# Attention with packed keys and a routed feed-forward: the second batch's routing read ahead of its last softmax steps, two subtractions on GpSimd

## The chip, the cores and the metric

The kernel runs on one core of one Trainium2 chip. The metric is the device time of one execution in microseconds, as the median of the runs shown. The profile is one such execution; its times are counted from the start of its span.

## The reference

Eight batches of 576 tokens with 8 heads of 64. An attention over 32 packed rows per head, then a top-1 mixture of experts on the result (D = 512, E = 8 experts, F = 1024):

```python
p_packed = sm_attn(p, k, v)              # 32 packed rows per head
out = sm_attn(q, p_packed, p_packed)     # softmax over the 32 rows
x = out.transpose(0, 2, 1, 3).reshape(B * S, H * D)
xn = x / (norm(x) + 1e-6); en = emb / (norm(emb) + 1e-6)
logits = xn @ en.T / tau
idx = argmax(logits, axis=1)             # the token's expert
gate = softmax(logits)[idx]
out[token] = gate * (relu(x @ w1[idx]) @ w2[idx])
```

## The kernel before

**Precision.** The feed-forward runs as fp32r with a high and a low part: `AT[:, 0]` is the attention's second softmax rounded (`high`, ScalarE), `AT[:, 1]` is the rest (`low`, one subtraction). The same split is made for the first weights times the packed rows (`G`, `w1_rows`, L854 and L855) and for the second weights (`w2s`, `split_w2`, L816 and L817). Each product takes three passes (`PASSES`).

**Batches and stages.** For each batch an expert is guessed from the sum of the logits, the whole batch is computed for it, and a loop behind it serves tokens that fall to another expert (with these inputs it has nothing to do). `ffn` is the backbone: for a batch it does two halves of the hidden layer (L923), the output of the tail tokens (L951, four times 24 matmuls), and that of the first 256 tokens (L969, two times 24). Between the pieces of `ffn` of batch b the steps of batch b + 1 are issued: attention part one (`att1`), the guess, `att2` (query scores, softmax, transposes), the routing (`route`), and then the keys of batch b + 2. While batch 0 is in `ffn`, a table of letters, `PLAN`, says after each yield of `ffn` what is issued: `a` a step of batch 1's attention, `r` one of batch 0's routing, `g` one of batch 0's gates, `w` a split of second weights. For later batches a rule does this.

**The softmax of att2** works on two halves of 288 tokens. For each: `unpack` (transposes out of PSUM), `biggest`, `shift`, `expo` on ScalarE, `total` (L597 to L599), `norm` (L603), `turn` (a transpose into `at`, L606), `high` (L609, ScalarE), `low` (L613). Its order stands in a list; for batch 1 (`early`) the list is rearranged a little.

**The routing** multiplies `at` with the packed rows and their logits (L681), in two groups of tokens: the first 256, all in the first half, with 32 matmuls, and the other 320 with 40. Each group fills both buffers `pt` of a PSUM pool that has two. A group is read tile by tile: VectorE sums the logits (L695), ScalarE squares the values and sums them up (L699). When the second group is read, the token's expert is found on VectorE (L706 to L723), and `counts` (L732, L735) sums it over the tokens on TensorE.

**The gates** (`gates`, L743 to L770) need an inverse root of the squares' sum. For batch 0 its three rounds (L102, L104, L111, L112) and two closing steps (L749, L750) run on GpSimd; VectorE, ScalarE (an exponential, L757) and VectorE again make the gate, and 16 small copies on ScalarE (L778) lay it out for the tail tokens, whose output L1267 multiplies.

**What the next batch needs.** `w1_rows` (L841) fills the same two `pt` buffers; each half is read by two casts on ScalarE (L854) and two subtractions on VectorE (L855). The key scores of batch b + 2 (L259) fill them again: the first four matmuls the one, the next four the other.

Every engine works through its instructions in the order in which they are issued.

Of the kernel before, what the change touches and what calls it, by code (L numbers as in the profile page):

```python
# [23 lines left out]
def kernel(  # L24
# [193 lines left out]
    def alternate(a, b):  # L218

        while a or b:  # L220
            for g in (a, b):
                if g:
                    try:
                        yield next(g)
                    except StopIteration:
                        a, b = (None, b) if g is a else (a, None)

    def idle(n):
        for _ in range(n):
            yield  # L230
# [317 lines left out]
    def att2(x, after=None, first=False, early=False):  # L548

        def eng(name, hf):  # L550
            i = ("S0", "S1", "N0", "N1", "L0", "L1").index(name + str(hf))
            if early and name + str(hf) in POOLED:
                return nc.gpsimd
            return nc.gpsimd if first and ENG[i] == "p" else nc.vector

        AT = sb.tile([P, 2, NG, S], F32R, name="AT", tag="AT")
        x.AT = AT
        NB = HS // 32
        both = slice(0, NG)
        sts, mxs, sums = [], [], []  # L560
        if first:
            at = x.at = sb.tile([P, NG, S], F32, name="at1", tag="ot", bufs=1)
        else:
            at = x.at = sb.tile([P, NG, S], F32, name="at", tag="at")

        def rows_of(t, gs):
            return t[:, gs].rearrange("p g (a j) -> p g a j", j=32)

        def spread(t, gs):
            n = gs.stop - gs.start  # L570
            return t[:, gs].unsqueeze(3).broadcast_to([P, n, NB, 32])

        def unpack(hf, gs=both):
            if gs.start == 0:
                sts.append(sb.tile([P, NG, HS], F32, name="st", tag="st", bufs=2))
            for g in range(gs.start, gs.stop):
                nc.vector.transpose(sts[hf][:, g], x.s2[hf][g])

        def biggest(hf, gs=both):
            if gs.start == 0:  # L580
                mxs.append(sm.tile([P, NG, NB], F32, name="mx2", tag="mx2", bufs=1))
            nc.vector.tensor_reduce(
                mxs[hf][:, gs], rows_of(sts[hf], gs), axis=AX.X, op=ALU.max
            )

        def shift(hf, gs=both):
            t = rows_of(sts[hf], gs)
            eng("S", hf).tensor_tensor(out=t, in0=t, in1=spread(mxs[hf], gs), op=ALU.subtract)  # L588

        def expo(hf, gs=both):  # L590
            nc.scalar.activation(sts[hf][:, gs], sts[hf][:, gs], AF.Exp, scale=SCALE)  # L591

        def total(hf, gs=both):
            if gs.start == 0:
                sums.append(sm.tile([P, NG, NB], F32, name="s2", tag="s2", bufs=1))
            t = sums[hf][:, gs]
            nc.vector.tensor_reduce(t, rows_of(sts[hf], gs), axis=AX.X, op=ALU.add)  # L597
            nc.vector.tensor_scalar(out=t, in0=t, scalar1=1e-9, scalar2=None, op0=ALU.add)
            nc.vector.reciprocal(t, t)  # L599

        def norm(hf, gs=both):
            t = rows_of(sts[hf], gs)
            eng("N", hf).tensor_tensor(out=t, in0=t, in1=spread(sums[hf], gs), op=ALU.mult)  # L603

        def turn(hf, gs=both):
            nc.vector.transpose(at[:, gs, hf * HS : (hf + 1) * HS], sts[hf][:, gs])  # L606

        def high(hf, gs=both):
            nc.scalar.copy(AT[:, 0, :, hf * HS : (hf + 1) * HS], at[:, :, hf * HS : (hf + 1) * HS])  # L609

        def low(hf, gs=both):
            cs = slice(hf * HS, (hf + 1) * HS)
            eng("L", hf).tensor_tensor(  # L613
                out=AT[:, 1, :, cs], in0=at[:, :, cs], in1=AT[:, 0, :, cs].bitcast(F32),
                op=ALU.subtract,
            )

        def softmax():
            order = (
                (unpack, 0), (biggest, 0), (shift, 0), (unpack, 1), (biggest, 1), (total, 0),  # L620
                (shift, 1), (norm, 0), (turn, 0), (total, 1), (low, 0), (norm, 1), (turn, 1),
            )
            if early:
                order = (order[0], order[3], order[1], order[2], *order[4:])
            if first:
                names = dict(
                    U=unpack, B=biggest, S=shift, X=expo, T=total, N=norm, R=turn, H=high, L=low
                )
                groups = {"": both, "a": slice(0, 1), "b": slice(1, 2)}
                order = [(names[t[0]], int(t[1]), groups[t[2:]]) for t in ORDS.split()]  # L630
            for step, hf, *gs in order:
                step(hf, *gs)
                if step is shift and not first:
                    expo(hf)
                if step is turn and not first and not hf:
                    high(hf)
                yield
            if first:
                return
            if not after:  # L640
                high(1)
                low(1)
                return
            high(1)
            yield from idle(1 if early else 4)
            steps = route(x)
            if early:
                yield next(steps)
                next(steps)
                yield next(steps)  # L650
                low(1)
                yield
                yield from steps
                yield from after
                return
            yield next(steps)
            next(steps)
            low(1)
            yield from idle(3)
            yield from alternate(after, steps)  # L660

        yield from softmax()


# [348 lines left out]
    order = {bi: n for n, bi in enumerate(seq)}  # L1013
# [220 lines left out]
    def store_main(b):  # L1234
# [60 lines left out]
        "qssq", "sssssssss", "sss", "ss", "ss", "ssG", "", "sG", "ssa", "ssa",  # L1295
# [5 lines left out]
    )  # L1301
    POOLED = ()
    DBL = 8
    LAG = 2

# [6 lines left out]
    with tc.manual_schedule():  # L1312
# [41 lines left out]
        for b in range(B):  # L1354
            after = bat[b + 1] if b + 1 < B else None
# [24 lines left out]
    with tc.If(n_rest > 0):  # L1380
        with tc.For_i(0, B, 1) as b:
            nb = nc.values_load(rest_i[0:1, ds(b, 1)], min_val=0, max_val=S)
            with tc.If(nb > 0):
                x = Batch()
# [98 lines left out]
```

## Time and profile before

| | us |
|---|---|
| median of 3 runs | 439.41 |
| the runs | 438.62, 439.89, 439.41 |
| the profiled execution | 438.68 |
| its span | 437.1 |
| TensorE (matmuls) busy | 417.7 |
| VectorE busy | 312.6 |
| ScalarE busy | 217.9 |
| GpSimd busy | 137.5 |

The profiled execution's mean granted TensorE clock is 0.985 of the full 2.4 GHz. A share of busy time is a mean over stages. The stage around this change lies between 60 and 95 us: batch 0 is in its output products, batch 1 in its softmax and routing. In the rows below PE is TensorE's matmuls, DVE VectorE, ACT ScalarE, POOL GpSimd; an instruction's idle time and what ended it stand in brackets.

### The profile page before, as it was taken

What the parts mean: (1) busy time and instruction counts of PE and PEld (TensorE: products, weight loads), DVE (VectorE), ACT (ScalarE), POOL (GpSimd) and SP (SyncE); (2) the same over time, 40 slices, a digit from 0 to 9 for tenths busy, and PEclk for the clock granted to TensorE, in tenths of its full rate; (3) what the DMA queues carried; (4) which work ended last, traced back from release to release, by engine and by line L of the source; (5) the groups of instructions that cost most, each with busy time, mean ns of one, the idle gap of its engine ahead of it and who ended that gap; (6) DMA issues with size and microseconds to landing.
All of it is one profiled execution on the core that took longest, in us unless ns stands there. A gap on an engine that the chain in (4) does not pass through costs nothing.

```text
span 437.1 us, 12609 instructions
## 1 busy us (share of the span) xinstructions
PE 417.7 (96%) x4802; PEld 351.7 (80%) x4803; DVE 312.6 (72%) x982; ACT 217.9 (50%) x652; POOL 137.5 (31%) x185
## 2 busy tenths in 40 slices
PE   7889996998999999999999999999999999999994
PEld 5646885688896889869896899859896898869993
DVE  4468678667996689868897589867897589656420
ACT  2456733665535744367534754367344664456300
POOL 2438743053212514044122424044041524035000
PEclk9899999799999999999999999999999999999998
DMA  7999989687897669965897668965798603731032
GB/s 198 294 292 281 247 232 264 189 188 172 251 359 206 152 192 305 310 167 128 249 362 204 153 178 270 326 180 135 215 335 246 170 16 102 287 74 36 2 63 53
DMA packets 47908, 88.36 MB, mean 202 GB/s; under 512 B 10904, under 2 KB 29400, under 8 KB 47840
## 3 DMA queue, kind: packets, MB, share of 16 engines
q1 hardware_dynamic: 39456, 57.83, 49.3%
q0 software_dynamic: 8000, 29.43, 19.5%
q8 instruction: 40, 0.66, 0.6%
q10 hardware_dynamic: 384, 0.21, 0.2%
q14 instruction: 28, 0.23, 0.2%
HBM read 78.00 MB, written 9.44 MB: 200 GB/s over the span
## 4 chain that ended last, share of the span: by engine, by line
PE 81%; DMA 7%; DVE 5%; ACT 3%; issue 1%; POOL 1%; SPq 1%; DVEq 0%; POOLq 0%; ACTq 0%
PE pf L951 24%; PE pf L969 19%; PE pf L923 19%; PE pt L259 4%; PE pt L681 4%; DMA nat<-in_v 3%; PE pt L841 3%; DMA nat<-in_q 2%; PE pt L384 2%; DMA nat<-in_k 2%; PE pt L364 1%; ACT scr L699 1%; PE pf L902 1%; PE pf L1179 1%; SPq L1251 1%
## 5 line engine op out<-in xcount | busy, mean ns | idle before, releaser
L817 POOL TENSOR_TENSOR w2s<-w2r,w2s 128x512 fp32r<-128x512 f32 x64 | 82.2, 1287 | 134.3 <-ACT w2s L816 133.0
L951 PE MATMUL pf<-hT,w2s 128*128 128x320 f32 x768 | 120.6, 312 | 0.0
L951 PEld LDWEIGHTS pf<-hT,w2s 128*128 128x128 f32 x768 | 113.0, 188 | 4.3 <-issue 3.3
L923 PE MATMUL pf<-AT,G 128*128 128x288 f32 x720 | 103.9, 298 | 0.1
L923 PEld LDWEIGHTS pf<-AT,G 128*128 128x128 f32 x720 | 97.3, 188 | 4.8 <-issue 2.3
L969 PE MATMUL pf<-w2s,hT 128*128 128x512 f32 (+1 forms) x408 | 96.7, 390 | 0.0
L969 PEld LDWEIGHTS pf<-w2s,hT 128*128 128x128 f32 x408 | 73.0, 191 | 20.8 <-issue 5.9
L926 DVE SCALAR_TENSOR_TENSOR hT<-pf,hT 128x288 fp32r<-128x288 f32 x128 | 56.3, 445 | 25.1 <-ACT hT L925 25.1
L925 ACT ACTIVATE hT<-pf 128x288 fp32r<-128x288 f32 x128 | 51.3, 415 | 39.2 <-PE pf L923 38.3
L699 ACT ACTIVATE scr<-pt 128x256 f32<-128x256 f32 (+1 forms) x80 | 29.8, 379 | 39.8 <-DVE lg L695 39.8
L816 ACT CAST w2s<-w2r 128x512 fp32r<-128x512 f32 x64 | 39.2, 624 | 6.3 <-issue 6.3
L792 POOL DMA_DIRECT2D w1t<-in_moe_w x14 | 10.7, 767 | 79.7 <-DVE st L588 75.1
L855 DVE TENSOR_TENSOR G<-pt,G 128x512 fp32r<-128x512 f32 x28 | 19.3, 690 | 17.4 <-ACT G L854 17.4
L778 ACT COPY gt<-gate 32x2 f32<-32x2 f32 (+1 forms) x128 | 24.6, 192 | 6.3 <-DVE gate L763 4.2
L1258 DVE STREAM_TRANSPOSE ot<-pf 128x320 f32<-128x320 f32 x32 | 16.0, 501 | 13.7 <-PE pf L951 11.5
L854 ACT CAST G<-pt 128x512 fp32r<-128x512 f32 x28 | 16.5, 589 | 17.6 <-DVE G L855 13.2
L609 ACT CAST AT<-at 128x576 fp32r<-128x576 f32 x16 | 10.8, 673 | 26.5 <-DVE at L606 25.4
L591 ACT ACTIVATE st<-st 128x576 f32<-128x576 f32 (+1 forms) x17 | 11.2, 658 | 24.0 <-issue 19.4
L681 PEld LDWEIGHTS pt<-ppf,at 32*64 32x64 f32 x1152 | 15.7, 136 | 8.9 <-ACT scr L699 4.4
L695 DVE TENSOR_REDUCE lg<-pt 128x8 f32<-128x32 f32 (+1 forms) x80 | 11.4, 175 | 15.8 <-PE pt L681 11.1
L681 PE MATMUL pt<-ppf,at 32*64 32x72 f32 x1152 | 18.4, 241 | 4.3 <-ACT scr L699 4.0
L289 DVE STREAM_TRANSPOSE kt<-nat 128x576 f32<-128x576 f32 x28 | 21.2, 762 | 0.0
(179 smaller groups left out, 491.9 us busy)
## 6 DMA issues: line engine op xcount, KB each, us to landing
nat<-in_k SPq DMA_DIRECT2D x112, 140.0 KB, 3.4
nat<-in_q SPq DMA_DIRECT2D x112, 140.0 KB, 5.0
w1t<-in_moe_w POOLq DMA_DIRECT2D x14, 1024.0 KB, 8.9
w2r<-in_moe_w POOLq DMA_DIRECT2D x28, 512.0 KB, 12.6
nat<-in_v SPq DMA_DIRECT2D x32, 160.0 KB, 3.8
out<-ot SPq DMA_DIRECT2D x28, 160.0 KB, 3.5
nat<-in_v SPq DMA_DIRECT2D x32, 128.0 KB, 3.7
out<-o SPq DMA_DIRECT2D x62, 64.0 KB, 1.7
```

The source lines that it names most:

```text
L289: nc.vector.transpose(kt.rearrange("p (n i) -> p n i", i=32), t)
L681: nc.tensor.matmul(pts[h // 2][64 * (n % 2) : 64 * (n % 2) + 64, at : at + XW], x.at[32 * h : 32 * h + 32, g, 64 * n : 64 * n + 64], x.ppf ...
L699: nc.scalar.activation(scr[:r], v[:, :, :D], AF.Square, accum_out=sss[:r, m, c : c + 1])
L778: copy(dst[32 * a : 32 * a + 32, k : k + HB * (n - 1) + 1 : HB], src[32 * k : 32 * k + 32, NCT : NCT + n],)
L816: nc.scalar.copy(hi, raw)
L817: eng.tensor_tensor(out=lo, in0=raw, in1=hi.bitcast(F32), op=ALU.subtract)
L855: nc.vector.tensor_tensor(out=x.G[:, 1, g, fs], in0=src, in1=x.G[:, 0, g, fs].bitcast(F32), op=ALU.subtract,)
L923: nc.tensor.matmul(pf[:, :HS], w, r, start=(n == 0), stop=(n == len(ops) - 1))
L925: nc.scalar.activation(hT[:, 0, f, cs], pf[:, :HS], AF.Relu)
L926: nc.vector.scalar_tensor_tensor(out=hT[:, 1, f, cs], in0=pf[:, :HS], scalar=0.0, in1=hT[:, 0, f, cs].bitcast(F32), op0=ALU.max, op1=ALU.s ...
L951: nc.tensor.matmul(pf[:, : S - TL], x.w2s[f][:, m, mt * P : mt * P + P], hT[:, a, f, TL:], start=(n == 0), stop=(n == len(ops) - 1),)
L969: nc.tensor.matmul(pf[:, :w], hT[:, a, f, c * P : (c + 1) * P], x.w2s[f][:, m, at : at + w], start=(f == 0 and i == 0), stop=(f == NF - 1 ...
```

## The change

For batch 1 alone, four things. The list of softmax steps ends before the last `norm` and `turn`; the routing's first group is issued and read there, and the two steps follow, then the second group. Both `low` subtractions go to GpSimd. In `PLAN` the steps of the gates of batch 0 (`g`) move, so that the gate's exponential and copies come behind the squares of batch 1. Some of the steps `a` come earlier or in twos and threes.

```diff
             if early:
-                order = (order[0], order[3], order[1], order[2], *order[4:])
+                order = (order[0], order[3], order[1], order[2], *order[4:9], *order[9:11])
...
             if first:
                 return
+            if early:
+                steps = route(x)
+                yield next(steps)
+                next(steps)
+                yield next(steps)
+                norm(1)
+                yield
+                turn(1)
+                high(1)
+                yield
+                yield next(steps)
+                low(1)
+                yield
+                yield from steps
+                yield from after
+                return
             if not after:
                 high(1)
                 low(1)
                 return
             high(1)
-            yield from idle(1 if early else 4)
+            yield from idle(4)
             steps = route(x)
-            if early:
-                yield next(steps)
-                next(steps)
-                yield next(steps)
-                low(1)
-                yield
-                yield from steps
-                yield from after
-                return
...
-        "ra", "ra", "ra", "ra", "a", "a", "ra", "ga", "ga", "ga",
-        "ga", "rga", "", "ga", "ga", "ga", "g", "ga", "gar", "ga",
-        "aa", "a", "a", "a", "a", "a", "a", "a", "", "",
+        "ra", "ra", "ra", "ra", "a", "a", "rga", "ga", "ga", "g",
+        "g", "", "", "aaa", "ar", "", "g", "", "aar", "aa",
+        "agg", "agggg", "a", "a", "a", "a", "", "", "", "",
     )
-    POOLED = ()
+    POOLED = ("L0", "L1")
```

`POOLED` names the softmax steps that batch 1 gives to GpSimd. Lines behind the first part are 7 higher in the changed kernel (L681 becomes L688).

How it moves instructions. TensorE, from the last products of the tail tokens on; `ppf,at` are batch 1's routing groups, `oh,ones` the counts of batch 0, `w1t,T` the next batch's first weights. Before:

```order
L681 MATMUL pt<-ppf,at 64x72 x32
L951 MATMUL pf<-hT,w2s 128x320 x8
L969 MATMUL pf<-w2s,hT 128x512 x6
L681 MATMUL pt<-ppf,at 64x72 x40
L969 MATMUL pf<-w2s,hT 128x512 x3
L732 MATMUL pu<-oh,ones 1x32
L735 MATMUL pu<-oh,ones 1x8
L969 MATMUL pf<-w2s,hT 128x512 x18
L841 MATMUL pt<-w1t,T 32x512 x16
```

and with the change:

```order
L688 MATMUL pt<-ppf,at 64x72 x32
L958 MATMUL pf<-hT,w2s 128x320 x8
L976 MATMUL pf<-w2s,hT 128x512 x9
L688 MATMUL pt<-ppf,at 64x72 x40
L739 MATMUL pu<-oh,ones 1x32
L742 MATMUL pu<-oh,ones 1x8
L976 MATMUL pf<-w2s,hT 128x512 x18
L848 MATMUL pt<-w1t,T 32x512 x16
```

The first group stays; the second comes three matmuls later and has the counts right behind it.

ScalarE, from the softmax's last exponential to the next batch's splits; `scr,ss` are the squares, `lgt` the gate's exponential, `gt` its copies. Before:

```order
L609 CAST AT<-at 128x2x288 x2
L757 ACTIVATE lgt<-lgt 128x40
L699 ACTIVATE scr,ss<-pt 128x256 x4
L778 COPY gt<-gate 32x3 x2
...
L699 ACTIVATE scr,ss<-pt 128x256 x2
L699 ACTIVATE scr,ss<-pt 64x256 x2
L816 CAST w2s<-w2r 128x512
L854 CAST G<-pt 128x512 x2
```

and with the change:

```order
L609 CAST AT<-at 128x2x288
L706 ACTIVATE scr,ss<-pt 128x256 x4
L609 CAST AT<-at 128x2x288
L764 ACTIVATE lgt<-lgt 128x40
L706 ACTIVATE scr,ss<-pt 128x256 x4
L706 ACTIVATE scr,ss<-pt 64x256 x2
L785 COPY gt<-gate 32x3 x2
...
L823 CAST w2s<-w2r 128x512
L861 CAST G<-pt 128x512 x2
```

The four squares of the first group pass the second `high` cast and the exponential; all 16 copies now stand behind all squares.

GpSimd, from the second round of the inverse root on. With the change:

```order
L112 TENSOR_TENSOR gy<-rq_t,gy 128x5
L613 TENSOR_TENSOR AT<-at,AT 128x2x288
L102 TENSOR_TENSOR rq_t<-rq_h,gy 128x5
L104 TENSOR_TENSOR rq_t<-rq_t,gy 128x5
L111 TENSOR_SCALAR rq_t<-rq_t 128x5
L112 TENSOR_TENSOR gy<-rq_t,gy 128x5
L756 TENSOR_TENSOR gy<-gy,sst 128x5
L757 TENSOR_SCALAR gy<-gy 128x5
L613 TENSOR_TENSOR AT<-at,AT 128x2x288
L714 TENSOR_TENSOR sst<-ss 128x5
```

Before, the two L613 were not in this queue; they stood on VectorE, in front of the last `norm` and behind the first group's logits.

## Rows read from the trace of the kernel before

**Rows 1.** Waits from 55 to 110 us: us in total, times, longest.

```profile
PE pt L681 <- ACT scr L699: 4.0, 1, 4.0
PE pt L384 <- DMA nat<-in_v: 1.2, 1, 1.2
```

**Rows 2.** Stretches: busy us of PE, PEld, DVE, ACT, POOL, then clock, DMA share, GB/s.

```profile
18.00:20.00 2.00, 2.00 (x17) 1.67 (x23) 0.69 (x1) 0.92 (x3) 0.00 (x0) 0.50 0.82 188
75.00:76.00 1.00, 0.00 (x0) 0.00 (x0) 0.48 (x4) 0.63 (x3) 0.00 (x0) 0.87 1.08 261
82.00:83.00 1.00, 1.00 (x5) 0.81 (x4) 0.80 (x4) 0.78 (x5) 0.14 (x1) 0.72 0.12 33
```

**Rows 3.** Timeline of PE: start us, us, instruction, count (records, two for some matmuls).

```profile
76.63 2.11 PE L681 MATMUL pt<-ppf,at 32*64 32x72 f32 x80 [4.01 <-ACT scr L699]
...
85.86 1.95 PE L841 MATMUL pt<-w1t,T 64*32 64x512 f32 x32
...
92.73 0.95 PE L923 MATMUL pf<-AT,G 128*128 128x288 f32 x6
...
93.78 1.28 PE L259 MATMUL pt<-kt,pw 64*32 64x288 f32 x30
...
132.68 5.15 PE L969 MATMUL pf<-w2s,hT 128*128 128x512 f32 x21
```

**Rows 4.** Chain of work that ended last, from 70 us on: start us, us.

```profile
73.80 0.24 POOL gy L750
...
75.19 0.20 DVE lg L695 x2
```

**Rows 5.** Timeline of DVE, 60 to 95 us.

```profile
69.99 0.69 DVE L613 TENSOR_TENSOR AT<-at,AT 128x576 fp32r<-128x576 f32 x1
70.61 0.74 DVE L603 TENSOR_TENSOR st<-st,s 128x576 f32<-128x576 f32 x1
71.39 0.78 DVE L606 STREAM_TRANSPOSE at<-st 128x576 f32<-128x576 f32 x1
72.09 0.23 DVE L711 TENSOR_SCALAR lgt<-lgt,itau 128x40 f32<-128x40 f32 x1
...
73.28 0.20 DVE L723 TENSOR_TENSOR oh<-code,lmx 128x40 f32<-128x40 f32 x1
73.41 0.50 DVE L1258 STREAM_TRANSPOSE ot<-pf 128x320 f32<-128x320 f32 x1
...
82.31 0.20 DVE L706 TENSOR_TENSOR lgt<-lg 128x40 f32<-128x40 f32 x1
...
85.99 0.78 DVE L1267 TENSOR_TENSOR ot<-ot,gt 128x640 f32<-128x640 f32 x1
...
89.40 0.65 DVE L855 TENSOR_TENSOR G<-pt,G 128x512 fp32r<-128x512 f32 x1
...
93.06 0.69 DVE L855 TENSOR_TENSOR G<-pt,G 128x512 fp32r<-128x512 f32 x1 [0.65 <-ACT G L854]
```

**Rows 6.** Timeline of POOL, 60 to 95 us, and L613 on POOL (ns min/median/max).

```profile
69.97 0.77 POOL L112 TENSOR_TENSOR gy<-rq_t,rq_i 128x5 f32<-128x5 f32 x1
70.81 0.59 POOL L102 TENSOR_TENSOR rq_t<-rq_h,gy 128x5 f32<-128x5 f32 x1
...
72.36 0.20 POOL L102 TENSOR_TENSOR rq_t<-rq_h,gy 128x5 f32<-128x5 f32 x1
...
L613 POOL TENSOR_TENSOR AT<-at,AT x2: 1399/1400/1401, 34.9 to 36.3; 128x576 fp32r<-128x576 f32 x2
```

**Rows 7.** Timelines of POOL and DVE about 138 us.

```profile
137.89 1.26 POOL L817 TENSOR_TENSOR w2s<-w2r,w2s 128x512 fp32r<-128x512 f32 x1 [15.62 <-ACT w2s L816]
...
138.02 1.19 DVE L723 TENSOR_TENSOR oh<-code,lmx 128x40 f32<-128x40 f32 x1
```

**Rows 8.** Timeline of ACT, 60 to 95 us.

```profile
72.20 0.67 ACT L609 CAST AT<-at 128x576 fp32r<-128x576 f32 x1 [2.83 <-DVE at L606]
...
76.84 2.42 ACT L778 COPY gt<-gate 32x3 f32<-32x3 f32 x12
```

More of the change, by code (lines that the diff above doesn't have):

```diff
@@ L639, in softmax @@
                 return
-            if not after:
-                high(1)
-                low(1)
-                return
-            high(1)
-            yield from idle(1 if early else 4)
-            steps = route(x)
             if early:
+                steps = route(x)
                 yield next(steps)
                 next(steps)
+                yield next(steps)
[4 more added lines that the diff above has]
+                yield
                 yield next(steps)
@@ L655, in softmax @@
                 return
+            if not after:
+                high(1)
+                low(1)
+                return
+            high(1)
+            yield from idle(4)
+            steps = route(x)
             yield next(steps)
```

## Prediction

> **What bounds the kernel now.** I read the waits between 55 and 110 us first, because TensorE (PE) is the engine that is nearly always busy and a change can only pay where PE stands. Two waits are long there: 4.0 us in front of the second routing group (L681) until ScalarE (ACT) has read the first group's squares, and 1.2 us on a load of v [rows 1]. The table of stretches shows a second cost of the first wait: the granted clock falls from 1.00 to 0.50 while PE stands (a mean of 0.87 from 75 to 76 us puts the fall at 75.75, some 3.1 us after PE's last matmul at 72.62) and returns at 82.55 (a mean of 0.72 from 82 to 83) [rows 2]. These are TensorE's two levels, 2.4 and 1.2 GHz. PE's timeline prices it: PE restarts at 76.63 and is busy from there on [rows 3], so of the 5.9 us to 82.55 half, 3.0, is lost to the low clock. With the stop of 4.0, **7.0 us is the most this change can give back at this place**.
>
> Why ACT was late is in the orders. The group's squares stand on ACT behind the exponential of the first batch's gates, which needs VectorE (DVE), which needs ten small GpSimd (POOL) steps; the last of these ends at 74.04 us in the chain of waits [rows 4]. The logits (L695) stand behind the same steps on DVE, at 75.19 [rows 4]. From there to PE's restart at 76.63 are 1.44 us.
>
> **The change, step by step.** The times below are those of the profiled execution with the change worked into it.
>
> 1. *First group read early.* Its PE place is unchanged. DVE is free for its logits where the low part's subtraction stood, at 69.99 [rows 5]; the transpose of an output tile (0.50, as L1258 at 73.41) comes first, so the logits start at 70.5 and, by the 1.44 us above, the banks are free at 71.9.
>
> 2. *Two subtractions (L613) go to POOL.* On DVE each is 0.69 [rows 5], on POOL 1.40 [rows 6]. DVE gains 1.4 us of room. POOL starts its small steps 0.7 earlier (the two integer steps pass a transpose of 0.78 on DVE) and is rid of two holds: its 0.2 us steps took 0.77 and 0.59 at 69.97 and 70.81, exactly while DVE ran L613 and L603 [rows 5, 6]. So its third round, which began at 72.36, would begin at 70.7 (0.7 and 0.96 less); the first subtraction stands there now and ends at 72.1.
>
> 3. *The hold works the other way too.* DVE's L723 on 128x40 needs 0.20 [rows 5], yet took 1.19 at 138.02, ending 0.06 after a POOL subtraction that ran from 137.89 to 139.15 [rows 7]. I take it as: a DVE step with two SBUF inputs that meets a running POOL step of that kind waits for its end. So the last normalisation (L603, 0.74), which DVE reaches at 71.9, starts at 72.1 and ends at 72.85; the last transpose (0.78) runs to 73.65. The Trainium skill (GPSIMD Engine Reference, Key points) says that GpSimd shares its SBUF interfaces with VectorE and contends with instructions of two SBUF inputs; it speaks against this change and does not say in which form. Were it a plain sharing of bandwidth, the small DVE steps would lose almost nothing and the sum would be that of the first rival; the rows show a full stop.
>
> 4. *PE at the second group.* PE was through six matmuls of L969 at 72.62 (76.63 less 4.01) and now has nine in front, at 5.15/21 = 0.245 each: 73.35 [rows 3]. The second half of the attention rows is there at 73.65, so PE stops 0.3 us instead of 4.0, and the clock stays. The group, 2.11 us at the low clock [rows 3], takes about 1.1 and ends at 74.8.
>
> 5. *The new wait: the counts.* The last high part on ACT starts 0.81 after its transpose began (71.39 to 72.20) and takes 0.67 [rows 5, 8], so 74.3. POOL's third round and closing steps take 1.68 (72.36 to 74.04) [rows 4, 6], and 0.65 more for the normalisation that holds them: 74.45. There the second subtraction starts and runs to 75.85. DVE's six one-hot steps begin 0.70 after the transpose's start and reach L723 1.19 later (71.39, 72.09, 73.28) [rows 5]: 74.75, inside that subtraction. L723 ends at 75.9, and the counts on PE, which were after the second group, wait for it: a stop of 1.1 us. Behind L723 on DVE stand the gates' reciprocal and product, an output transpose and the counts' sum, some 1.0 us, and only then the second group's logits: 76.9.
>
> 6. *DVE's chain to the next batch.* Six logits paced by six ACT squares are 2.2 us (1.44 x 6/4), three gate steps 0.7: DVE reaches L706 at 79.8, against 82.31 [rows 5]. From L706 to the first split of the next batch's first weights (L855) were 7.09 us [rows 5]. The sixteen gate copies, now in one piece behind the squares, take 16 x 2.42/12 = 3.2 us on ACT [rows 8], from 79.6 to 82.8; DVE, with one key tile (0.8) less in front, is at the output product (L1267) 2.9 us after L706 (85.99 less 82.31 less 0.8) [rows 5], at 82.7. It waits 0.1 to 0.3. So L855 starts at 87.1 and the fourth of them, 4.35 us later (89.40 to 93.06 plus 0.69) [rows 5], ends at 91.4.
>
> 7. *PE there.* From 75.95 with counts 0.2, 18 L969 4.4, then 6.87 (85.86 to 92.73) and 1.05 (92.73 to 93.78) [rows 3], PE is at the next batch's key scores (L259) at 88.5. The first four write a bank that is free; the next need the bank that the fourth split releases, at 91.5. PE stops about 2.5 to 3 us in two pieces. Before, it came there at 93.8, just after the split's end at 93.75. **Gain 2.4 us**, counting 0.14 for the four that are done.
>
> What is behind that point keeps its distances: PE's next stop, 1.2 us on v [rows 1], hangs on DVE steps behind the key scores, so it moves along. The list of waits shows none on the next batch's weights, whose use comes some 6 us earlier on PE now, and SyncE's queue keeps its order. From 110 us on PE has no stop to speak of, so the gain reaches the end.
>
> Bounds. The held POOL time on DVE's path: between nothing (gain 4.0) and both subtractions in full (2.8, gain 1.2). I take 1.6, since the meetings fall as worked out in 3 and 5. The profiled execution's own time is 438.68, 0.73 under the median of the three runs, 439.41. The sum gives 436.2 against the first and 437.0 against the second; I forecast **436.6**.
>
> **The rivals.**
> - *No hold worth naming.* The subtractions fall between DVE's steps, DVE's chain is 1.5 us earlier, gain 4.0: 435.0. For it: many DVE steps (transposes, reductions, those that read PSUM) run beside POOL unhindered. Against: the meetings are computed at both places. Chance 0.13. The full 7.0 (432.4) would need DVE's chain to be 3 us earlier still: 0.04.
> - *The clock falls at the key scores.* The new stop of 2.5 to 3 us is almost as long as the 3.1 us after which it fell before; and from 18 to 20 us the clock was 0.50 while PE is shown busy throughout, behind a stretch of very small matmuls, so a full stop isn't needed [rows 2]. Against: the new stop is a little shorter and comes in two pieces with matmuls between them. Price from half to all of the 3.0 us above: 438.1 to 439.6, taken as 438.6. Chance 0.24.
> - *GpSimd becomes the bound, slower.* DVE's chain waits for POOL's ten small steps. If those behind the first subtraction are each held by a DVE step as the two seen were (0.57 and 0.39 more, so 6 x 0.48 = 2.9), the second subtraction ends near 78.8 and everything of 5 and 6 is 2.9 later: key scores at 94.4, no gain left. The stop at the key scores is then 5.5 us, the clock falls too, and 3.0 are added: 442. It decides from 2.4 us of lateness on; the clock from about 0.5. Against it: DVE has few steps of two SBUF inputs in that stretch. Chance 0.07.
>
> **How the numbers follow.** The forecast with a gain of 1.5 to 3.2 us has 0.50, its own range 435.6 to 437.9; 0.13 and 0.04 lie below, 0.24 and 0.07 above, 0.02 is for what I don't see. A measurement of this kernel tells 0.3% (1.3 us) from no change. Faster by more: 0.50 + 0.13 + 0.04 and a part of the clock rival, 0.73. Within: the rest of the clock rival, 0.20. Slower: 0.07. The range from 434.6 to 438.9 leaves out the full gain, the upper end of the clock rival and the slower case.
>
> **What would show it.** Right: PE's wait for L681 in that stretch under 0.6 us and the clock 1.00 from 73 to 80; the first squares on ACT before 72; both L613 on POOL near 1.4; a small one-hot step on DVE of about 1 us; a stop in front of the counts near 1 us and one of 2 to 3 in front of the next batch's key scores, ended by DVE's last split. Wrong: no stop at the key scores (then the gain is larger), a clock of 0.50 behind it, or POOL's last closing step later than 75.

## The result and the profile after

The kernel after takes 434.34 us (median of four runs, 433.53 to 434.41), the kernel before 439.01 (four runs, 438.19 to 439.89): a ratio of 0.9896, with a 95% interval from 0.9872 to 0.9920. The forecast was 436.6 us, with a range from 434.6 to 438.9: the direction was right, the gain was nearly twice the forecast, and the time fell 0.3 us below the range.

The profiled execution after took 434.29 us, with a span of 432.7 against 437.1. Line numbers behind the changed function are 7 higher (L681 is L688, L855 is L862, L1267 is L1274). First TensorE's waits from 55 to 110 us in the kernel after:

```profile
PE pt L259 <- DVE hit L1238: 1.3, 1, 1.3
PE pu L739 <- DVE oh L730: 0.9, 1, 0.9
PE pu L532 <- ACT ppf L433: 0.3, 1, 0.3
PE pt L384 <- issue: 0.2, 1, 0.2
PE pf L930 <- DVE G L862: 0.2, 1, 0.2
```

The wait of 4.0 us for L681 is gone; in its place stand 0.9 us in front of the counts and 1.3 in front of the next batch's key scores, the two places that were forecast. But the wait on v, 1.2 us before [rows 1], is gone too (0.2 are left), and that was not forecast. TensorE's timeline after:

```profile
60.28 1.21 PE L688 MATMUL pt<-ppf,at 32*64 32x72 f32 x80
...
73.91 1.23 PE L688 MATMUL pt<-ppf,at 32*64 32x72 f32 x80
76.06 0.22 PE L739 MATMUL pu<-oh,ones 128*1 128x32 f32 x2 [0.92 <-DVE oh L730]
...
88.92 0.40 PE L930 MATMUL pf<-AT,G 128*128 128x288 f32 x1 [0.20 <-DVE G L862]
...
91.35 1.17 PE L259 MATMUL pt<-kt,pw 64*32 64x288 f32 x24 [1.26 <-DVE hit L1238]
92.46 5.80 PE L930 MATMUL pf<-AT,G 128*128 128x288 f32 x42
...
103.60 0.90 PE L384 MATMUL pt<-nat,p1T 128*32 128x64 f32 x40 [0.22 <-issue]
...
289.44 1.57 PE L259 MATMUL pt<-kt,pw 64*32 64x288 f32 x30
290.94 1.32 PE L930 MATMUL pf<-AT,G 128*128 128x288 f32 x8
```

And the same places of the kernel before, with batch 0's second routing group, ahead of the change:

```profile
59.97 1.21 PE L681 MATMUL pt<-ppf,at 32*64 32x72 f32 x80
...
95.00 5.80 PE L923 MATMUL pf<-AT,G 128*128 128x288 f32 x42
...
107.10 0.90 PE L384 MATMUL pt<-nat,p1T 128*32 128x64 f32 x40 [1.18 <-DMA nat<-in_v]
...
292.94 0.67 PE L259 MATMUL pt<-kt,pw 64*32 64x288 f32 x6
294.28 1.17 PE L259 MATMUL pt<-kt,pw 64*32 64x288 f32 x24 [0.67 <-DVE cnt L737]
295.39 1.85 PE L923 MATMUL pf<-AT,G 128*128 128x288 f32 x12
```

Read as differences, the two timelines place the gain in three steps. At the products behind the key scores TensorE is **2.54 us** earlier (95.00 to 92.46), where 2.4 was forecast. Behind the load of v it is 3.50 earlier (107.10 to 103.60): **0.96 more**. There it stays until 292.94, where the kernel before has one more stop that the kernel after has not; behind it the lead is 4.45 (295.39 to 290.94): **0.95 more**. The spans differ by 4.4.

The first step needs a correction, because the two executions do not enter the stage together. Batch 0's second routing group, which the change does not move, begins at 59.97 before and at 60.28 after. In the second profiles of the same two kernels it begins at 60.60 and 60.22, so a shift of this size comes with the execution and not with the change. Counted from that group, the first step is **2.85** (35.03 and 32.18 us), the other two stay, and the whole is 4.7, as in the medians (4.67).

Now the engines that set the first step. VectorE after:

```profile
70.69 0.25 DVE L702 TENSOR_REDUCE lg<-pt 128x8 f32<-128x32 f32 x2
...
71.92 1.03 DVE L603 TENSOR_TENSOR st<-st,s 128x576 f32<-128x576 f32 x1
...
74.88 1.13 DVE L730 TENSOR_TENSOR oh<-code,lmx 128x40 f32<-128x40 f32 x1
...
76.77 0.27 DVE L702 TENSOR_REDUCE lg<-pt 128x8 f32<-128x32 f32 x2
...
82.03 0.20 DVE L286 STREAM_TRANSPOSE kt<-nat 128x64 f32<-128x64 f32 x1
82.69 0.82 DVE L1274 TENSOR_TENSOR ot<-ot,gt 128x640 f32<-128x640 f32 x1 [0.46 <-ACT gt L785]
...
86.87 0.65 DVE L862 TENSOR_TENSOR G<-pt,G 128x512 fp32r<-128x512 f32 x1
...
90.52 0.69 DVE L862 TENSOR_TENSOR G<-pt,G 128x512 fp32r<-128x512 f32 x1 [0.65 <-ACT G L861]
```

GpSimd after:

```profile
70.90 1.44 POOL L613 TENSOR_TENSOR AT<-at,AT 128x576 fp32r<-128x576 f32 x1
72.29 0.71 POOL L102 TENSOR_TENSOR rq_t<-rq_h,gy 128x5 f32<-128x5 f32 x1
...
74.24 0.23 POOL L757 TENSOR_SCALAR gy<-gy 128x5 f32<-128x5 f32 x1
74.55 1.40 POOL L613 TENSOR_TENSOR AT<-at,AT 128x576 fp32r<-128x576 f32 x1
```

The first group's logits start at 70.69 (forecast 70.5). Both subtractions are on GpSimd at 1.4, the normalisation L603 is held to 1.03 (0.74 alone) and GpSimd's L102 then by L603 (0.71 for 0.20); the second subtraction starts at 74.55 (forecast 74.45) and L730 is held to 1.13 (forecast 1.15). The second group's logits follow at 76.77 (76.9), the last split ends at 91.21 (91.4).

SyncE's queue explains the second step. The listing gives start, time and count of its issues; first the kernel before, then the kernel after:

```profile
85.31 4.66 SPq L174 DMA_DIRECT2D nat<-in_q  x8
90.06 1.79 SPq L200 DMA_DIRECT2D nat<-in_v  x4
91.90 0.43 SPq L1278 DMA_DIRECT2D out<-ot  x1
...
97.03 3.84 SPq L1251 DMA_DIRECT2D out<-o  x8
100.97 3.11 SPq L200 DMA_DIRECT2D nat<-in_v  x4
```

```profile
82.26 4.53 SPq L174 DMA_DIRECT2D nat<-in_q  x8
86.88 1.79 SPq L200 DMA_DIRECT2D nat<-in_v  x4
88.71 0.43 SPq L1285 DMA_DIRECT2D out<-ot  x1
...
93.81 3.84 SPq L1258 DMA_DIRECT2D out<-o  x8
97.74 2.67 SPq L200 DMA_DIRECT2D nat<-in_v  x4
```

From the first key tile's last transpose on (82.03 plus 0.20 after) the issues stand end to end: eight loads of q, four of v, eight stores of the tail, eight of the output, and only then the second tile of v, which TensorE waits for. That load's last issue ends at 104.08 before and 100.41 after, 3.67 us earlier, while TensorE comes only 2.54 earlier. So the wait shrinks away.

### The profile page after: what moved, and what is told of

It reads as the page before. It is cut to its first block, busy times and chain, and to the rows that moved or that the text cites. A ratio compares the mean times of both kernels' runs of the same rounds, so it can differ in the third digit from the quotient of the medians.

```text
span 432.7 us, 12610 instructions
## 1 busy us (share of the span) xinstructions
PE 418.4 (97%) x4802; PEld 352.0 (81%) x4803; DVE 311.4 (72%) x980; ACT 217.6 (50%) x652; POOL 139.8 (32%) x187
## 4 chain that ended last, share of the span: by engine, by line
PE 85%; DVE 5%; DMA 4%; ACT 3%; issue 1%; POOL 0%; DVEq 0%; SPq 0%; ACTq 0%
PE pf L958 24%; PE pf L930 21%; PE pf L976 19%; PE pt L259 4%; PE pt L688 3%; PE pt L848 3%; PE pt L384 2%; DMA nat<-in_q 2%; DMA nat<-in_v 2%; PE pt L364 2%; PE pf L1107 1%; ACT scr L706 1%; PE pt L237 1%; PE pf L909 1%; PE pf L1186 1%
## 5 line engine op out<-in xcount | busy, mean ns | idle before, releaser
L976 PE MATMUL pf<-w2s,hT 128*128 128x512 f32 (+1 forms) x408 | 94.8, 385 | 0.0
L976 PEld LDWEIGHTS pf<-w2s,hT 128*128 128x128 f32 x408 | 72.0, 188 | 20.5 <-issue 5.9
L862 DVE TENSOR_TENSOR G<-pt,G 128x512 fp32r<-128x512 f32 x28 | 19.3, 690 | 17.4 <-ACT G L861 17.4
L1248 ACT ACTIVATE o<-pf,gate 128x512 f32<-128x512 f32 (+1 forms) x17 | 11.3, 667 | 18.8 <-issue 14.3
L807 POOL DMA_DIRECT2D w2r<-in_moe_w x28 | 19.7, 711 | 0.0
```

Source lines behind the costliest of these rows:

```text
L807: queue.dma_start(t, w2e[:, 2 * i : 2 * i + 2, :])
L862: nc.vector.tensor_tensor(out=x.G[:, 1, g, fs], in0=src, in1=x.G[:, 0, g, fs].bitcast(F32), op=ALU.subtract,)
L976: nc.tensor.matmul(pf[:, :w], hT[:, a, f, c * P : (c + 1) * P], x.w2s[f][:, m, at : at + w], start=(f == 0 and i == 0), stop=(f == NF - 1 ...
```

## The experiments

**The kernel before again.** No edit.

> The kernel before once more, for a second profile. Theory: the stop of 1.2 us on v near 106 us and the wait of about 1.7 us in SyncE's issues at 101 us belong to the program and come again within 0.3 us. The stop of 0.67 us in front of the key scores near 294 us, which the kernel after does not have, is the meeting of two VectorE steps (L718, L723) with one GpSimd subtraction. If it belongs to the program, it is here again and is worth 0.5 to 0.7 us of the gain; if it is chance of one execution, it is under 0.2 us here.

Measured: 439.03 us, span 437.4. Stops 4.0 in front of L681, 1.0 on v, and 0.67 near 294.7 us again. The second load of v again has one long issue (1.67 us, the others about 0.4). So the stop at 294 us is no chance of one execution. What makes it are two steps of VectorE and two subtractions of GpSimd in the kernel before:

```profile
286.57 1.29 DVE L718 SCALAR_TENSOR_TENSOR oh<-lgt,code 128x40 f32<-128x40 f32 x1
...
288.13 1.13 DVE L723 TENSOR_TENSOR oh<-code,lmx 128x40 f32<-128x40 f32 x1
```

```profile
286.54 1.27 POOL L817 TENSOR_TENSOR w2s<-w2r,w2s 128x512 fp32r<-128x512 f32 x1 [15.73 <-ACT w2s L816]
...
287.93 1.28 POOL L817 TENSOR_TENSOR w2s<-w2r,w2s 128x512 fp32r<-128x512 f32 x1
```

L718 comes 0.03 us after GpSimd's subtraction has begun and is held; L723 runs into the next one and is held as well. In the kernel after, L725 (the former L718) starts at 282.71, 0.33 before the subtraction at 283.04, and only the last of the three is held (1.19). A shift of 0.4 us between two engines, 200 us behind the change, decides over one held step more. All fourteen profiles bear this out: in five, L718 (L725) begins 0.03 or 0.04 us behind the subtraction and takes 1.28 or 1.29, and in each of these the stop is there; in the other nine it takes 0.20, and the stop is in none.

**The tail's stores off SyncE's queue, in the kernel before.**

```
-                    nc.sync.dma_start(rs[0][:, NCB // 2 - 1], t[:, 0])
-                    nc.sync.dma_start(rs[1], t[:, 1:])
+                    nc.gpsimd.dma_start(rs[0][:, NCB // 2 - 1], t[:, 0])
+                    nc.gpsimd.dma_start(rs[1], t[:, 1:])
```

> The kernel before, with the eight stores of the first batch's tail (L1278, L1279) issued by GpSimd and not by SyncE. Theory 1 (the 1.2 us stop on v comes from SyncE's queue, whose issues stand end to end from 85 to 104 us, eight of them these stores): the last load of v is issued 4 to 5 us earlier, the stop near 106 us falls from 1.2 to under 0.3 us, and the kernel is 0.8 to 1.2 us faster than before (ratio 0.997 to 0.998). Theory 2 (the load waits for VectorE's steps behind the key scores, as the prediction had it): the stop stays 1.0 to 1.3 us and the time is within 0.3 us of before. The 4.0 us stop in front of L681 stays in both.

Measured: 437.81 us, ratio 0.9971 (0.9957 to 0.9986). The stop on v is gone, L384 runs in one piece:

```profile
106.21 1.73 PE L384 MATMUL pt<-nat,p1T 128*32 128x64 f32 x80
```

The load of v ends its issues at 100.42 (98.60 plus 1.82) instead of 104.08, though SyncE's queue began 0.9 later, as the whole stage did in this execution. Theory 1 holds: SyncE's queue sets the wait on v. (The stop at 294 us is absent here too, so this run's gain is not v's alone.)

**Only the gates moved.** Four lines of the order's table in the kernel before:

```
-        "ra", "ra", "ra", "ra", "a", "a", "ra", "ga", "ga", "ga",
-        "ga", "rga", "", "ga", "ga", "ga", "g", "ga", "gar", "ga",
-        "aa", "a", "a", "a", "a", "a", "a", "a", "", "",
+        "ra", "ra", "ra", "ra", "a", "a", "rga", "ga", "ga", "ga",
+        "ga", "ra", "", "a", "a", "a", "g", "a", "ar", "a",
+        "ggaa", "gggga", "a", "a", "a", "a", "a", "a", "", "",
```

> The kernel before, with only the gates of the first batch moved: exponential behind the first group's squares, all sixteen copies behind the second group's. The first group's reading is not moved ahead of the last softmax steps. Theory 1 (the stop in front of the second group has two parts: the gates cost 1.2 to 1.5 us of it, VectorE's and ScalarE's late reading the rest of 4.0): the stop falls from 4.0 to 2.4 to 2.9 us, the clock stays 1.00 (it fell 3.1 us after the last matmul), and the key scores of the next batch are held by VectorE's splits as in the kernel after; 435.0 to 437.0 us, that is 2 to 4 us faster than before. Theory 2 (the gates are not in the way, the low part's subtraction and the last softmax steps are): the stop stays above 3.5 us, the clock falls to 0.50, and the time is within 1 us of before.

Measured: 436.91 us, ratio 0.9955 (0.9938 to 0.9973). The stop fell from 4.0 to 2.5, as theory 1 had it. The rest of it failed: no split of VectorE held the key scores (they ran from 92.90 on without a stop), and the clock fell all the same:

```profile
78.00:79.00 1.00, 1.00 (x7) 0.55 1.01 261
...
81.00:82.00 1.00, 1.00 (x5) 0.74 1.02 377
```

(columns: busy time of PE, granted clock, DMA share, GB/s). It fell near 78.1 us, 1.5 us after TensorE had started again at 76.58. Counted from batch 0's second routing group, the products behind the key scores come at 32.89, 2.1 us earlier than before (35.03); the stop at 294 us is still there (near 292 here).

**The early reading with the gates at their old places.** The `g` letters of the table go back; the two subtractions stay on GpSimd. The gate factor meets logits that are not shifted yet, so the gates come out with other values, and the variant is read for its time alone.

```
-        "ra", "ra", "ra", "ra", "a", "a", "rga", "ga", "ga", "g",
-        "g", "", "", "aaa", "ar", "", "g", "", "aar", "aa",
-        "agg", "agggg", "a", "a", "a", "a", "", "", "", "",
+        "ra", "ra", "ra", "ra", "a", "a", "ra", "ga", "ga", "g",
+        "g", "g", "", "gaaa", "gar", "g", "g", "g", "gaar", "gaa",
+        "a", "a", "a", "a", "a", "a", "", "", "", "",
```

> The kernel after, with the first batch's gates back at their old places in the order: exponential on ScalarE in front of the first group's squares, the copies in front of the second group's. The gate factor is applied to the logits before they are shifted, so the gates' values differ. Theory 1 (the early reading alone gives little, since ScalarE's squares stand behind the exponential and this behind GpSimd's ten steps): the stop in front of the second group is 2.0 to 3.5 us instead of 0, key scores 1 to 2.5 us later than in the kernel after, the clock falls to 0.50 at one of the two stops: 435.5 to 438.0 us. Theory 2 (the early reading is what counts): the stop is under 0.5 us and the time within 0.7 us of the kernel after.

Measured: 440.84 us, ratio 1.004 (1.0017 to 1.0063): slower than the kernel before, and by more than theory 1 gave.

```profile
PE pt L688 <- DVE lgt L718: 4.5, 1, 4.5
```

```profile
75.60 0.19 DVE L759 RECIPROCAL gy<-gy 128x5 f32<-128x5 f32 x1 [3.90 <-POOL gy L757]
```

VectorE stands 3.9 us on GpSimd's ten small steps and on the first subtraction among them (1.43 us from 71.38), with the last normalisation, its transpose and the one-hot steps queued behind it; in the kernel before, those stood ahead and ran in that time [rows 5]. The clock then fell to 0.50 from 79.5 to 86.4. So the early reading does not pay with the gates in its way; how much of its loss is the subtraction's was not tried apart. The gates alone bring less than half of the whole by the medians (1.7 of 4.7 us), but in the profile most of what is gained at the key scores (2.1 of 2.85). Neither part is the change.

**Both subtractions back on VectorE, in the kernel after.**

```
-    POOLED = ("L0", "L1")
+    POOLED = ()
```

> The kernel after, with both low-part subtractions (L613) back on VectorE. Theory 1 (the hold: a VectorE step of two SBUF inputs that meets a running GpSimd step stands until that ends): the last normalisation L603 takes 0.74 again and not 1.03, the one-hot step L730 0.20 and not 1.13, so 1.2 us come back against 1.2 to 1.4 us for the two subtractions; within 0.5 us of the kernel after. Theory 2 (no hold, the long steps have another cause, and moving them to GpSimd was worth their full 1.4 us): L603 and L730 stay long and the time is 1.0 to 1.4 us above the kernel after, about 435.7.

Measured: 435.97 us, ratio 0.9936 (0.9915 to 0.9958). No VectorE step between 68 and 82 us takes over 0.9 us, so the two holds are GpSimd's subtractions, as theory 1 says. The stop in front of the counts is gone, but L848 then takes 2.8 us instead of 1.95, and the key scores restart at 91.06 against 91.35, or 31.18 and 31.07 us behind batch 0's second routing group: on TensorE's path the subtractions' place changes 0.1 us. The time is 1.6 us above the kernel after, and not within 0.5 as theory 1 had it. It comes near theory 2's 435.7, but by something else: the stop at 291 us (0.65) is back, and in the profiled execution (436.5 us) the clock fell at the key scores, 0.61, 0.50, 0.50 and 0.69 of full speed in the four microseconds from 91 to 95. Whether it fell in the others, no trace shows.

**That variant again.**

> The variant with both subtractions on VectorE once more, for a second profile. If the fall of the clock near 91.5 us is chance per execution, it need not come again here; if that variant's activity decides it, it does. The stop of 0.65 us in front of the key scores near 291 us should come again, since it came in both profiles of the kernel before and in none of the two of the kernel after.

Measured: 435.3 us, span 433.6. The clock stayed at 1.00 behind the same stop of 1.26; the key scores restart at 91.44, and the stop at 291 us came again. So without a fall of the clock it is 1.0 us above the kernel after, about what the stop at 291 us costs (0.95 above).

**The kernel after again.**

> The kernel after once more, for a second profile and more times on one chip. Three readings of the 2.0 us that it was faster than my sum: (1) the smaller stop on v (0.2 against 1.2 us): it belongs to the program, since SyncE's queue starts from the first key tile, 3.0 us earlier while TensorE is 2.5 us earlier; here again 0.0 to 0.4 us. (2) The stop in front of the key scores near 290 us (0.7 us in the kernel before and in its repeat, none after): if the program decides it, none here either; if chance does, 0.7 us and about 435.0 us in the profiled run. (3) The clock at the key scores near 91 us: it stayed 1.00 in the kernel after, but fell to 0.50 for 3 us in the variant with both subtractions on VectorE, after the same stop of 1.26 us; if it is chance per run, some runs here are 1.4 to 1.6 us longer than others, and the times spread over 433.5 to 436.

Measured: 434.56 us (433.81 to 437.74), ratio 0.9901 (0.9873 to 0.9928). No stop on v, none at 290 us. In its profiled execution, 435.36 us, the clock fell at the key scores:

```profile
91.00:92.00 1.00, 0.73 (x20) 0.52 (x24) 0.44 (x4) 1.00 (x3) 0.43 (x1) 0.93 0.79 181
92.00:93.00 1.00, 1.00 (x9) 0.19 (x2) 0.06 (x1) 0.90 (x3) 1.00 (x2) 0.50 0.68 156
```

against the first profile of the same kernel, after the same stop:

```profile
91.00:92.00 1.00, 0.65 (x20) 0.52 (x24) 0.52 (x4) 1.00 (x4) 0.34 (x1) 1.00 0.73 179
92.00:93.00 1.00, 1.00 (x19) 0.54 (x5) 0.00 (x0) 0.99 (x3) 1.00 (x2) 1.00 0.72 138
```

(busy time of PE, TensorE's weight loads, DVE, ACT, POOL, then the clock, DMA share and GB/s). TensorE is 1.46 us later at L364 (99.56 against 98.10) and 1.17 later behind the load of v, since the 0.2 there is saved. That no stop on v shows is partly luck: the load's last issue ends 1.46 us later than in the first profile as well (101.87 against 100.41), and meets a TensorE that the clock has made as late.

**The output product on GpSimd, in the kernel after.**

```
-                nc.vector.tensor_tensor(
+                (nc.vector if b else nc.gpsimd).tensor_tensor(
```

> The kernel after, with the first batch's output product (L1274, twice) on GpSimd and not on VectorE. Theory 1 (VectorE's chain to its last split ends the stop in front of the key scores, and behind it the load of v is next): VectorE's chain is 1.9 us shorter, the stop of 1.26 us at the key scores goes (under 0.3 us), TensorE is there 1.2 to 1.5 us earlier, but SyncE's queue still starts from the first key tile at 82.2 us, so the load of v lands at 103.4 us as before and TensorE stops there for 1.2 to 1.6 us: within 0.5 us of the kernel after. Theory 2 (TensorE's place decides when the load of v is issued): no stop on v, 1.2 to 1.5 us faster than the kernel after, about 433. Theory 3 (GpSimd's products hold VectorE's splits L862, which read SBUF too): the stop stays above 1 us and the time is the same or up to 1.5 us above after.

Measured: 435.68 us (433.72 to 437.45), ratio 0.9920 (0.9896 to 0.9943); span of the profile 432.8 against 432.7.

```profile
90.07 5.80 PE L930 MATMUL pf<-AT,G 128*128 128x288 f32 x42
...
103.82 0.90 PE L384 MATMUL pt<-nat,p1T 128*32 128x64 f32 x40 [2.83 <-DMA nat<-in_v]
```

Theory 1, with larger sizes: the stop at the key scores is gone and TensorE is 2.4 us earlier there (90.07 against 92.46), and all of it is lost on v, which arrives when it did (103.82 against 103.60). SyncE's queue still began at 82.24. This is the plainest proof that TensorE's place does not move the load. The median is 1.1 us above the repeat of the kernel after on the same chip (434.56), which theory 1 did not have; the intervals of the two overlap, and the profile is of one of the faster executions (434.50).

**That, and the tail's stores on GpSimd's queue** (the edit of the stores shown above as well).

> The one before it, and the eight stores of the tail (L1285, L1286) issued by GpSimd and not by SyncE as well. Theory 1: the load of v is issued 4 to 5 us earlier and the stop on it is under 0.2 us; the gain at the key scores now reaches the end: 1.2 to 1.6 us faster than the kernel after, 432.8 to 433.2 us. Theory 2 (GpSimd becomes late: its subtractions for the second weights stand behind eight issues of some 0.6 us each, and TensorE's products wait for them): a new stop of 1 us or more on w2s, and no gain.

Measured: 438.53 us, ratio 0.998 (0.997 to 0.9991): the gain is lost, as theory 2 had it, but by a mechanism that neither had.

```profile
88.72 7.28 DVE L1238 TENSOR_TENSOR hit<-cnt,sel 1x8 f32<-1x8 f32 x1
```

```profile
90.72 5.25 POOL L824 TENSOR_TENSOR w2s<-w2r,w2s 128x512 fp32r<-128x512 f32 x4
```

A VectorE step on eight numbers, 0.14 us in the kernel after, is held for 7.28: through the rest of GpSimd's issues and all four subtractions that had piled up behind them. TensorE then stands 4.4 us, and the clock is at 0.50 from 94.3 to 101.1. In the run with the stores moved in the kernel before, the same step came while three subtractions stood in a row and got in behind the first (0.68 us), so a pile does not always hold it to its end.

**The load of v ahead of the stores, in the kernel after.** Once the last key tile is turned, its buffer is free and the load can go.

```
-            yield from keys(bat[b], nat_main(b), pns[b])
+            for n, _ in enumerate(keys(bat[b], nat_main(b), pns[b])):
+                if b == 2 and n == NPR:
+                    prefetch(order[b, NPR - 1] + 6)
+                yield
```

> The kernel after, with one load moved on SyncE's queue: the next batch's second tile of v is issued as soon as the last key tile has been turned, ahead of the sixteen stores and not behind them. Theory (in the kernel after, SyncE's queue and VectorE's splits are nearly level, the splits a little later): the stop of 0.2 us on v goes and nothing else, so 0 to 0.3 us faster than the kernel after, 434.0 to 434.5 us. If the load of v were the real bound of the kernel after, 1 us or more would come.

Measured: 434.14 us, ratio 0.9892 (0.9872 to 0.9911): the stop on v is gone, and nothing more comes, as expected.

**Both: the product on GpSimd and the load of v early.**

> The kernel after with both: the output product on GpSimd, and the second tile of v issued ahead of the stores. Theory (two bounds stand side by side: VectorE's chain to its last split ends at 91.2 us, SyncE's queue puts v at 103.4 us; taking away the first alone only lengthened the stop on v from 0.2 to 2.8 us): neither stop is left, TensorE runs from the counts to 110 us without one, 2.2 to 2.8 us faster than the kernel after: 431.7 to 432.3 us, and the runs stand closer together since there is no stop at which the clock can fall. Rival: the next load behind it (keys of the batch after) comes late in its place, under 1 us of gain.

Measured: 432.22 us (431.73 to 432.69), ratio 0.9841 (0.9826 to 0.9855), the best of the study with the next one; 1.9 us under the one above on the same chip. From 55 to 110 us TensorE keeps two waits, 0.9 us in front of the counts (L739) and 0.3 at L532; neither the key scores nor the load of v stops it any more.

**That, with both subtractions on VectorE.**

> The one before it, with both low-part subtractions (L613) back on VectorE. Theory (GpSimd's subtraction holds VectorE for as long as VectorE saves, and with the first weights of the next batch landing near 82 us an earlier TensorE only waits there): no stop in front of the counts, but the gain is lost at L848; within 0.4 us of the one before it. Rival (VectorE's room is worth it): 0.7 to 1.4 us slower.

Measured: 431.92 us (430.88 to 433.63), ratio 0.9847 (0.9824 to 0.9871): no difference that can be told. TensorE is at L848 1.5 us earlier (80.13 against 81.67), but 1.0 of that it already was at batch 0's second routing group (60.24 against 61.21); the other 0.6 and more is lost in L848, which takes 3.1 us instead of 2.0. What it waits for there the trace does not show.

## Why the prediction was right and wrong

*Steps 1 to 7 came true*, nearly all within about 0.5 us: the early logits, the price of the subtractions on GpSimd, the hold in both directions, the closed stop with the clock at 1.00, the new waits of 0.9 and 1.3 us, VectorE's last split as the end of the second, and a gain of 2.54 us at the key scores for the forecast 2.4 (2.85 from batch 0's second routing group, so the nearness of 2.54 is partly luck). The length of the stop there was off, 1.26 us and not 2.5 to 3, because TensorE came to the first key scores 0.9 later than I had it (89.4 for 88.5): the last product ahead of them, at 88.92, waits for VectorE's second split, which I had not counted. The end of the stop, on which the gain hangs, was right (91.35 for 91.5). (438.68 less 2.4 is 436.3, not the 436.2 of the sum; nothing hangs on it.)

The runs bear out the reasons: without GpSimd's subtractions the holds vanish, and without the output product on VectorE the stop at the key scores does. The Trainium skill (SBUF — State Buffer, Who interferes with whom) says of the hold what I took from [rows 7]: a VectorE instruction with two SBUF inputs contends with a GpSimd instruction that reads SBUF, the shared interface is an exclusive lock, and the order of issue decides who waits. The trace agrees: L730 takes 1.13 instead of 0.20 when it comes second, GpSimd's L102 0.71 instead of 0.20 when it does.

*The step that failed* is the sentence behind step 7: "What is behind that point keeps its distances: PE's next stop, 1.2 us on v, hangs on DVE steps behind the key scores, so it moves along." It took the place of the load from the list of waits; the load hangs on SyncE's queue, whose 28 issues ahead of it start with the *first key tile*, not behind the key scores. That start moved by 3.05 us (85.31 to 82.26), the splits and TensorE by 2.5. The 0.5 between them is VectorE's new wait of 0.46 in front of the output product, which the change had put behind the first key tile: it delays the splits and not the queue. The other 0.6 of the 3.67 are two long issues within the queue (1.52 and 1.69 us before, 1.38 and 1.27 after). So the wait on v fell by 0.96. With the queue read rightly but my own time for it, the sum would have moved it by a tenth or so only; the label was wrong, and the size came from two small terms that I did not have. The second of them is chance: in the second profiles the same 32 issues took 18.64 us before and 19.70 after, against 18.77 and 18.15 in the first. With the load taken out of that place altogether the median is 434.14, so on the whole the stop on v is nearly gone in the kernel after.

*The second term that was missing*, 0.95 us at 294 us, stands in the kernel before's list of waits behind 110 us, as 0.7 us. I wrote that "from 110 us on PE has no stop to speak of" and had not asked whether that stop hangs on a meeting of the two engines which any shift may undo. It was there in both profiles of the kernel before, in that with its gates moved, and in both of the kernel after with only the subtractions back on VectorE (0.65 to 0.67 us). It was not in the kernel before with the stores moved, nor in the kernel after or its other variants. Since it goes or stays with edits that do not touch that place, I call its 0.95 us luck of this change and no merit of its mechanism. What shifts the engines against each other by 0.4 us there stays open; it was not tried.

*The rivals.* "The clock falls at the key scores" is neither true nor false: with the same stop of 1.26 us it fell in two of six profiles (the second of the kernel after, the first with the subtractions on VectorE), and cost TensorE 1.46 us there and the kernel after 1.1 net (435.36 against 434.29), at or under the lower end of the 1.5 to 3.0. Of the four runs of the result only the profiled one, without a fall there, has a trace; the other three lie within 0.8 us of it. "No hold" is refuted by [rows 7] and by the two profiles that lose the holds with the subtractions. "GpSimd becomes the bound" did not happen here (the last closing step ended at 74.47, forecast 74.45), but the run with the gates at their old places shows what it costs: VectorE stood 3.9 us on GpSimd's last closing step, and the kernel took 440.84. The full 7.0 us stayed out of reach at this place: with the product on GpSimd and v early, the products behind the key scores are 5.2 us ahead (29.82 against 35.03 from batch 0's second routing group). The rest of that run's 6.8 us under its kernel before are the stops on v and at 294 us.

## What to carry to other kernels

When one stop is closed, write down for the next stop which queue releases it and from which instruction that queue starts, and move that start, not the consumer: a queue of issues that stand end to end ahead of a load is a bound of its own, and two bounds that are level (VectorE's splits and SyncE's queue here) must be moved together, since either one alone brought nothing that can be measured and both together 1.9 us. Parts of such a change must be tried apart before they are kept: here one half alone brought 1.7 us, the other half alone lost 1.6, together they brought 4.7 (about 1 of it luck). Take care with what lets two-input steps pile up on GpSimd: a VectorE step on two SBUF inputs waited for a whole pile in one run here (7.28 us), and for one of three in another. And before two profiles are subtracted, compare them ahead of the change: here executions of one kernel differed by 0.6 us there.

## What was not expected of the hardware

A VectorE step of two SBUF inputs can be held by several GpSimd instructions in a row, 7.28 us for a step of 0.14, not only by the one that runs when it comes; in another run the same step got in behind the first of three (0.68 us), and what decides stays open. The granted clock can fall after TensorE is at work again: near 91.9 us in the second profile of the kernel after, 0.6 us after its restart at 91.27, and 1.5 us after the restart in the run with the gates late; in the kernel before it fell 3.1 us after the last matmul and inside the stop [rows 2]. The same stop of 1.26 us left it at 1.00 in four of six profiles, and so did a stop of 2.83 us on v in the run with the product on GpSimd. And single issues on SyncE take 1.1 to 1.8 us instead of 0.3 to 0.7, on other transfers in each execution; from the first load of q to the last issue of v the same 32 issues took 17.2 to 18.8 us in eight profiles and 19.7 in the second of the kernel after.
